# Chunked attention with a gated feed-forward: batch 0 in wide rows turned on the tensor engine, eight heads per step, shared PSUM banks and a hand-written order

## The chip, the cores and the metric

The kernel runs on one core of one Trainium2 chip. The metric is the device time in microseconds (us) of one execution. Each execution has a state: "fast" or "slow" (more than 1.5% above the fastest of the same kernel), and "unknown" for a kernel that ran only once. The profile is of one execution and has its own clock, and all moments below are us from the start of its span. The profile of the kernel before has a span 4 us below the median of the times in the table.

## The reference

There are two stages. The first is an attention in chunks of 32 tokens; each chunk sees 16 tokens to its left, itself, 8 tokens to its right, and 8 memory tokens. The second is a feed-forward layer (FFN below) with a ReLU gate.

```python
# q, k, v: [4 batches, 8 heads, 768 tokens, 64], float32; mem_k, mem_v: [4, 8, 8, 64]
for c in range(768 // 32):
    q_c    = q[:, :, 32*c : 32*c+32]
    k_full = concat(mem_k, k[:, :, max(0, 32*c-16) : min(768, 32*c+40)])
    v_full = concat(mem_v, v[:, :, same range])
    out[:, :, 32*c : 32*c+32] = softmax(q_c @ k_full.T / 8) @ v_full
x = out.transpose(0, 2, 1, 3).reshape(3072, 512)
y = (relu(x @ w_gate) * (x @ w_val)) @ w_out     # w_gate, w_val: [512, 1536]; w_out: [1536, 512]
```

## The kernel before

The 3072 tokens are cut into 8 blocks of 384; blocks 0 and 1 are batch 0. A block passes through these stations: q, k and v are loaded in float32; VectorE (DVE) casts them to 16 bits; one DMA transpose each makes kT and qT (head dimension on the partitions); the attention of four steps of 96 queries makes x; four DMA transposes make xT; then the FFN runs on TensorE (PE): twelve units of 4 gate and 4 value matmuls (384 columns each), then three output projections of 12 matmuls (512 columns).

```python
# PSUM: scores 2 banks, values 1, gate and value 4, output 1
sps = tile_pool(name="sps", bufs=2, PSUM); pps = tile_pool(name="pps", bufs=1, PSUM)
fps = tile_pool(name="fps", bufs=4, PSUM); ops = tile_pool(name="ops", bufs=1, PSUM)

def src(self, t, h0, nh, tok, parts):          # one token of one head: 64 floats = 256 bytes in a row
    return bass.AP(tensor=t.tensor, offset=t[self.b, h0, tok, 0].offset,
                   ap=[[D, parts], [S * D, nh], [1, D]])
def turn_k(self, h0, nh):                      # turn_q is alike
    nc.sync.dma_start_transpose(self.kT[...], self.kn[...])

# ... cut: start of the program ...
b0 = blocks[0]
for h0 in (0, 4):
    b0.load_k(h0, 4, sp); b0.load_q(h0, 4, nc.scalar.dma_start); b0.load_v(h0, 4, sp)
nc.gpsimd.tensor_copy(gate, b0.qf[:, 0, 4, 0:1])    # POOL waits for q, then issues all weights
for c in range(0, DFF, 512):
    pool(w_gate_sb[...]); pool(w_val_sb[...])
for c in range(0, NDC, 4):
    pool(w_out_sb[...])
# ... cut: casts, transposes and attention of block 0; load_all(blocks[1]) after its first four heads ...

# steady state: while the FFN of block n runs, block n+1 has its attention,
# block n+2 is loaded at the start, and cast and turned at units 8 to 13
for n in range(NBLK):
    ffn = ffn_units(blocks[n]); att = attention(blocks[n + 1], order)
    load_all(blocks[n + 2]); steps = prep_steps(blocks[n + 2])
    for u in range(len(ffn)):
        if 2 <= u < 2 + len(att): att[u - 2][1]()
        if u < len(att):          att[u][0]()
        ffn[u]()
        if u in steps:            steps[u]()
```

The raw tiles of q, k and v have two buffers each. The order on each engine is not simply that of the text: a scheduler sets it.

The softmax here doesn't subtract the row's maximum and nothing guards it: scores larger than these inputs give would overflow.

Of the kernel before, what the change touches and what calls it, by code (L numbers as in the profile page):

```python
# [7 lines left out]
F32 = mybir.dt.float32  # L8
F16 = mybir.dt.float16
BF16 = mybir.dt.bfloat16  # L10
# [6 lines left out]
def kernel(  # L17
# [18 lines left out]
    QB = 96  # L36
# [12 lines left out]
    MEMCOL = 400  # L49

    wpool = ctx.enter_context(tc.tile_pool(name="wpool", bufs=1))
    vpool = ctx.enter_context(tc.tile_pool(name="vpool", bufs=2))
    tpool = ctx.enter_context(tc.tile_pool(name="tpool", bufs=2))
    rpool = ctx.enter_context(tc.tile_pool(name="rpool", bufs=4))
    xpool = ctx.enter_context(tc.tile_pool(name="xpool", bufs=6))
# [3 lines left out]
    opool = ctx.enter_context(tc.tile_pool(name="opool", bufs=3))  # L59

    sps = ctx.enter_context(tc.tile_pool(name="sps", bufs=2, space=bass.MemoryType.PSUM))
    pps = ctx.enter_context(tc.tile_pool(name="pps", bufs=1, space=bass.MemoryType.PSUM))
    fps = ctx.enter_context(tc.tile_pool(name="fps", bufs=4, space=bass.MemoryType.PSUM))
    ops = ctx.enter_context(tc.tile_pool(name="ops", bufs=1, space=bass.MemoryType.PSUM))



    qn_t = [wpool.tile([128, HP, 2, NT, 2 * D], BF16, name=f"qn{i}") for i in range(2)]
    kf_t = [wpool.tile([128, 4, H, D], F32, name=f"kf{i}") for i in range(2)]
    vb_t = [wpool.tile([128, NJ, H, VW], F16, name=f"vb{i}") for i in range(3)]  # L70
    vf_t = [wpool.tile([128, NJ, H, D], F32, name=f"vf{i}") for i in range(2)]
    memv = wpool.tile([NMEM, B * H, D], F32, name="memv")
    ex_t = [wpool.tile([128, 4, 128], F16, name=f"ex{i}") for i in range(3)]
    for i in range(2):
        nc.vector.memset(kf_t[i][:, 3], 0.0)
    for i in range(2):
        nc.vector.memset(qn_t[i], 0.0)
    for t in vf_t:
        nc.gpsimd.memset(t[0:NMEM], 0.0)
    for t in ex_t:  # L80
        nc.gpsimd.memset(t[:, :, QB:128], 0.0)
    for t in vb_t:
        nc.gpsimd.memset(t[:, :, :, D:VW], 1.0)
# [3 lines left out]

    def build_mask(name, qb):

        m = wpool.tile([128, QB], F16, name=name)  # L90
        nc.gpsimd.memset(m, 1.0)
        bs = q_band_start(qb) - NMEM
        for g in range(QB // 32):
            c = 3 * qb + g
            lo = max(32 * c - 16, 0) - bs
            hi = min(32 * c + 40, S) - bs
            sl = m[:, 32 * g:32 * g + 32]
            if lo > NMEM:
                nc.gpsimd.affine_select(
                    out=sl, in_=sl, pattern=[[0, 32]], compare_op=ALU.is_ge,  # L100
                    fill=0.0, base=-lo, channel_multiplier=1,
                )
            if hi < 128:
                nc.gpsimd.affine_select(
                    out=sl, in_=sl, pattern=[[0, 32]], compare_op=ALU.is_ge,
                    fill=0.0, base=hi - 1, channel_multiplier=-1,
                )
        nc.gpsimd.memset(m[0:NMEM], 1.0)
        return m
# [6 lines left out]
    w_gate_sb = wpool.tile([128, NFC, DFF], F16, name="w_gate_sb")  # L116
    w_val_sb = wpool.tile([128, NFC, DFF], F16, name="w_val_sb")
    w_out_sb = wpool.tile([128, NDC, DM], F16, name="w_out_sb")

    class Block:  # L120


        def __init__(self, n):
            self.n, self.b, self.T = n, n // 2, n % 2
            self.kbase = 0 if self.T == 0 else MB - 16
            self.starts = [q_band_start(NJ * self.T + j) for j in range(NJ)]
            self.qn, self.kf = qn_t[n % 2], kf_t[n % 2]
            self.vb = vb_t[n % 3]
            self.qf = vpool.tile([128, NT, H, D], F32, name="qf")
            self.vf = vf_t[n % 2]  # L130
            self.kn = vpool.tile([128, HP, 4, 2 * D], BF16, name="kn")
            self.qT = tpool.tile([128, HP, 2, NT, 128], BF16, name="qT")
            self.kT = tpool.tile([128, HP, KCOLS], BF16, name="kT")
            self.kb = tpool.tile([128, HP, NJ, 128], BF16, name="kb")
            self.xT = None

        def src(self, t, h0, nh, tok, parts):
            return bass.AP(
                tensor=t.tensor, offset=t[self.b, h0, tok, 0].offset,
                ap=[[D, parts], [S * D, nh], [1, D]],  # L140
            )

        def load_k(self, h0, nh, dma):
            hs = slice(h0, h0 + nh)
            for t in range(3):
                dma(self.kf[:, t, hs, :], self.src(k, h0, nh, self.kbase + 128 * t, 128))  # L146
            dma(self.kf[0:16, 3, hs, :], self.src(k, h0, nh, self.kbase + 384, 16))
            dma(self.kf[16:24, 3, hs, :], bass.AP(
                tensor=mem_k.tensor, offset=mem_k[self.b, h0, 0, 0].offset,
                ap=[[D, NMEM], [NMEM * D, nh], [1, D]]))  # L150

        def load_q(self, h0, nh, dma):
            hs = slice(h0, h0 + nh)
            for t in range(NT):
                dma(self.qf[:, t, hs, :], self.src(q, h0, nh, MB * self.T + 128 * t, 128))

        def load_v(self, h0, nh, dma):
            hs = slice(h0, h0 + nh)
            for j in range(NJ):
                dma(self.vf[NMEM:128, j, hs, :], self.src(v, h0, nh, self.starts[j], BAND))  # L160

        def cast_k(self, h0, nh):
            p0, p1 = h0 // 2, (h0 + nh) // 2
            nc.vector.tensor_copy(
                self.kn[:, p0:p1], self.kf[:, :, h0:h0 + nh, :].rearrange("p t (a x) d -> p a t (x d)", x=2))

        def cast_q(self, h0, nh):
            p0, p1 = h0 // 2, (h0 + nh) // 2
            view = self.qf[:, :, h0:h0 + nh, :].rearrange("p t (a x) d -> p x a t d", x=2)
            for x in range(2):  # L170
                nc.vector.tensor_copy(self.qn[:, p0:p1, x, :, D * x:D * x + D], view[:, x])

        def cast_v(self, h0, nh):
            nc.vector.tensor_copy(self.vb[:, :, h0:h0 + nh, 0:D], self.vf[:, :, h0:h0 + nh, :])  # L174
            m = memv[:, H * self.b + h0:H * self.b + h0 + nh, :]
            m4 = bass.AP(tensor=m.tensor, offset=m.offset, ap=[m.ap[0], [0, NJ], [D, nh], [1, D]])
            nc.gpsimd.tensor_copy(self.vb[0:NMEM, :, h0:h0 + nh, 0:D], m4)  # L177

        def turn_k(self, h0, nh):
            p0, p1 = h0 // 2, (h0 + nh) // 2  # L180
            nc.sync.dma_start_transpose(  # L181
                self.kT[:, p0:p1].rearrange("p a (t c) -> p (a t) c", c=128),
                self.kn[:, p0:p1].rearrange("p a t c -> p (a t c)"))

        def turn_q(self, h0, nh):
# [20 lines left out]

    n_exp = [0]

    def quad_stages(blk, j, g, x_big):
        st = {}  # L210

        def scores():
# [179 lines left out]
```

## Time and profile before

| | before |
|---|---|
| time, median of 2 runs | 298.62 us (297.70 to 299.54) |
| span of the profile | 294.4 us |
| first gate matmul of block 0 | 72.2 us |
| first gate matmul of block 2 | 131.2 us |
| first gate matmul of block 4 | 184.4 us |
| a middle block | 26.2 to 26.9 us |

The page of the profile cuts the span into 40 equal slices (7.4 us each). A digit is the busy share of a slice in tenths; "DMA" is the mean over the 16 DMA engines; "GB/s" is what they moved. Three lines of it, and the line of the busiest group: line of the kernel, engine, operation, output and inputs, count, busy time in us, mean ns of one, and the idle time before them with what ended it.

```profile
PE   0000002147999799989999999999999499999983
...
DMA  9999999997929877899499989969896611111001
GB/s 166 217 197 187 195 145 207 233 181 168 218 51 171 207 163 157 135 243 239 92 205 246 217 121 237 225 136 193 223 245 119 139 71 28 29 51 59 0 36 71
...
L269 PE MATMUL g_ps<-xT,w_gate_sb 128*128 128x384 f16 x384 | 81.9, 328 | 0.4 <-DMA xT<-x_big 0.4
```

There are two regimes. For the first ten slices DMA is full and PE almost idle; then PE is full and DMA nearly so, until the loads end around slice 31. What PE waited for (total us, times, longest us) shows the same: the first scores waited until 44.8 us for the transposed q.

```profile
PE s_ps L215 <- DMA qT<-qn_94: 47.6, 3, 44.8
PE o_ps L231 <- DVE x_big L236: 10.7, 6, 7.4
```

Each line is a stretch of the span: its length, then for each engine the busy time and the number of instructions, the granted clock, the DMA share, and GB/s. The DMA share is worked out from the time that packets took. In a crowded stretch they took longer: the median of the 256-byte packets of SP's queue is 31 ns from 16 to 40 us, with the weights of POOL's queue beside them, and 18 ns from 52 to 76 us, without. There the share can come out above 1 (1.23 in the second line below).

```profile
core 0: us, PE busy (x) PEld busy (x) DVE busy (x) ACT busy (x) POOL busy (x), PEclk, DMA share, GB/s
0.00:184.40 184.40, 118.45 (x781) 66.80 (x782) 88.27 (x223) 51.50 (x103) 27.88 (x50) 0.99 0.97 184
22.00:38.00 16.00, 0.00 (x0) 0.10 (x1) 1.26 (x4) 0.00 (x0) 1.52 (x4) 1.00 1.23 191
131.20:158.10 26.90, 26.25 (x181) 15.00 (x180) 16.30 (x44) 11.48 (x24) 1.89 (x1) 1.00 0.91 199
```

From 22 to 38 us the share is 1.23, so a crowded stretch hides idle time elsewhere. A plainer count comes from the packet records of the kept trace (it is not a view of the page): up to 184.4 us at least one packet was under way for 165.9 us, and none for 18.5 us.

### The profile page before, as it was taken

To read this page: it belongs to the slowest core of one execution; us is meant where nothing else is said; L and a number is where in the kernel's file an instruction comes from. 1 tells how busy PE (TensorE), PEld (TensorE's weight loads), DVE (VectorE), ACT (ScalarE), POOL (GpSimd) and SP (SyncE) were. 2 spreads that over 40 slices of the span, in tenths; PEclk is the share of its full clock that TensorE was granted. 3 is DMA by queue.
4 is the path that set the end of the run, shared out by engine and by line. 5 is a ranking of instruction groups with operands and counts; after the bars stand their busy time and mean duration, and the time that the engine had idled before them with its cause. 6 is when DMAs were issued, how large, how long until landed. Compare 5 with 4: busy or idle time off the path is not lost.

```text
span 294.4 us, 4093 instructions
## 1 busy us (share of the span) xinstructions
PE 219.2 (74%) x1440; PEld 123.4 (42%) x1440; DVE 140.4 (48%) x355; ACT 92.9 (32%) x185; POOL 31.7 (11%) x52
## 2 busy tenths in 40 slices
PE   0000002147999799989999999999999499999983
PEld 0000001024554266546545654664565256545641
DVE  4400103675584079429924971884398127612310
ACT  1000002023342165236424622642453136423411
POOL 7950200020002000200020020002002000000000
PEclk9999999999999799999999999999999999999999
DMA  9999999997929877899499989969896611111001
GB/s 166 217 197 187 195 145 207 233 181 168 218 51 171 207 163 157 135 243 239 92 205 246 217 121 237 225 136 193 223 245 119 139 71 28 29 51 59 0 36 71
DMA packets 146152, 45.82 MB, mean 156 GB/s; under 512 B 138436, under 2 KB 143044, under 8 KB 146132
## 3 DMA queue, kind: packets, MB, share of 16 engines
q1 hardware_dynamic: 138164, 39.99, 67.1%
q0 software_dynamic: 4800, 4.79, 9.7%
q10 hardware_dynamic: 3168, 0.79, 1.5%
q8 instruction: 11, 0.18, 0.2%
q14 instruction: 9, 0.07, 0.1%
HBM read 30.34 MB, written 6.29 MB: 124 GB/s over the span
## 4 chain that ended last, share of the span: by engine, by line
PE 62%; DMA 21%; SPq 8%; DVE 5%; issue 1%; ACT 1%; ACTq 0%; DVEq 0%
PE vl_ps L273 20%; PE g_ps L269 19%; PE out_ps L284 16%; DMA vf_101<-in_v_dram 5%; DMA qT<-qn_94 5%; DMA qT<-qn_95 5%; PE o_ps L231 4%; PE s_ps L215 4%; DMA qf<-in_q_dram 3%; SPq L146 3%; DMA kf_96<-in_k_dram 2%; SPq L187 2%; SPq L181 1%; DVE gvT L277 1%; DMA xT<-x_big 1%
## 5 line engine op out<-in xcount | busy, mean ns | idle before, releaser
L269 PE MATMUL g_ps<-xT,w_gate_sb 128*128 128x384 f16 x384 | 81.9, 328 | 0.4 <-DMA xT<-x_big 0.4
L273 PE MATMUL vl_ps<-xT,w_val_sb 128*128 128x384 f16 x384 | 80.1, 329 | 0.0
L277 DVE TENSOR_TENSOR gvT<-vl_ps,g_relu 128x384 f16<-128x384 f32 x96 | 53.3, 555 | 54.3 <-PE vl_ps L273 53.0
L284 PE MATMUL out_ps<-w_out_sb,gvT 128*128 128x512 f16 x288 | 67.5, 385 | 1.6 <-ACT o_sb L287 1.3
L215 PE MATMUL s_ps<-qT,kb 128*128 128x192 bf16 x128 | 23.1, 272 | 58.4 <-DMA qT<-qn_94 47.6
L276 ACT ACTIVATE g_relu<-g_ps 128x384 f16<-128x384 f32 x96 | 47.2, 492 | 49.0 <-PE g_ps L269 31.9
L273 PEld LDWEIGHTS <-w_val_sb 128*128 128x128 f16 x384 | 37.6, 98 | 24.6 <-issue 0.7
L284 PEld LDWEIGHTS <-gvT 128*128 128x128 f16 x288 | 28.5, 99 | 36.4 <-issue 6.6
L269 PEld LDWEIGHTS <-w_gate_sb 128*128 128x128 f16 x384 | 35.7, 98 | 18.8 <-issue 1.6
L215 PEld LDWEIGHTS <-kb 128*128 128x128 bf16 x128 | 11.6, 105 | 64.4 <-DVE kb L204 40.8
L287 ACT COPY o_sb<-out_ps 128x512 f32<-128x512 f32 x24 | 14.1, 587 | 63.1 <-PE out_ps L284 63.1
L236 DVE TENSOR_TENSOR x_big<-o_ps,rinv 96x256 f16<-96x256 f32 x64 | 26.7, 418 | 1.2
L222 ACT ACTIVATE ex_104<-s_ps 128x384 f16<-128x384 f32 x22 | 10.8, 493 | 46.0 <-PE s_ps L215 44.6
L222 ACT ACTIVATE ex_105<-s_ps 128x384 f16<-128x384 f32 x21 | 10.3, 492 | 21.8 <-PE s_ps L215 20.9
L222 ACT ACTIVATE ex_106<-s_ps 128x384 f16<-128x384 f32 x21 | 10.3, 492 | 12.6 <-PE s_ps L215 11.9
L177 POOL CAST vb_99<-memv 8x2048 f16<-8x2048 f32 x3 | 5.7, 1903 | 75.9 <-DVE vb_99 L174 75.9
L177 POOL CAST vb_98<-memv 8x1024 f16<-8x1024 f32 (+1 forms) x4 | 5.8, 1458 | 64.0 <-DVE vb_98 L174 64.0
L234 DVE RECIPROCAL rinv<-o_ps 96x4 f32<-96x4 f32 x64 | 11.0, 171 | 3.2 <-PE o_ps L231 2.9
L201 DVE COPY kb<-kT 128x1440 bf16<-128x1440 bf16 (+1 forms) x9 | 4.8, 531 | 15.6 <-DMA kT<-kn 15.6
L174 DVE CAST vb_98<-vf_101 128x1024 f16<-128x1024 f32 (+1 forms) x3 | 2.6, 868 | 15.9 <-DMA vf_101<-in_v_dram 15.9
L231 PEld LDWEIGHTS <-ex_105 128*128 128x128 f16 x84 | 4.9, 103 | 11.9 <-DVE x_big L236 10.5
L177 POOL CAST vb_100<-memv 8x2048 f16<-8x2048 f32 x2 | 3.8, 1886 | 54.1 <-DVE vb_100 L174 54.1
(65 smaller groups left out, 107.6 us busy)
## 6 DMA issues: line engine op xcount, KB each, us to landing
out_dram<-o_sb SPq DMA_DIRECT2D x24, 256.0 KB
qf<-in_q_dram SPq DMA_DIRECT2D x21, 256.0 KB
vf_102<-in_v_dram SPq DMA_DIRECT2D x16, 240.0 KB
kf_97<-in_k_dram SPq DMA_DIRECT2D x12, 256.0 KB
vf_101<-in_v_dram SPq DMA_DIRECT2D x12, 240.0 KB
kf_96<-in_k_dram SPq DMA_DIRECT2D x9, 256.0 KB
w_gate_sb<-in_moe_w_gate_dram POOLq DMA_DIRECT2D x3, 512.0 KB, 10.3
w_val_sb<-in_moe_w_val_dram POOLq DMA_DIRECT2D x3, 512.0 KB, 12.7
```

The source lines that it names most:

```text
L177: nc.gpsimd.tensor_copy(self.vb[0:NMEM, :, h0:h0 + nh, 0:D], m4)
L215: nc.tensor.matmul(s_ps[:, i], lhsT=blk.kb[:, 2 * g + i, j, :], rhs=blk.qT[:, 2 * g + i].rearrange("p x t c -> p x (t c)")[:, :, QB * j:QB ...
L222: nc.scalar.activation(e, s_ps.rearrange("p a x c -> p (a x) c"), ACT.Exp, scale=SCALE)
L231: nc.tensor.matmul(o_ps[:, i, :], lhsT=st["ex"][:, i, :], rhs=blk.vb[:, j, 4 * g + i, :], start=True, stop=True)
L234: nc.vector.reciprocal(rinv, o_ps[0:QB, :, D:D + 1])
L236: nc.vector.tensor_tensor(out=x_big[:, 256 * g:256 * g + 256].rearrange("p (h d) -> p h d", h=4), in0=o_ps[0:QB, :, 0:D], in1=rinv_b, op=A ...
L269: nc.tensor.matmul(g_ps, lhsT=w_gate_sb[:, f, 128 * m:128 * m + 128], rhs=blk.xT[:, f, :], start=(f == 0), stop=(f == NFC - 1))
L273: nc.tensor.matmul(vl_ps, lhsT=w_val_sb[:, f, 128 * m:128 * m + 128], rhs=blk.xT[:, f, :], start=(f == 0), stop=(f == NFC - 1))
L276: nc.scalar.activation(g_relu, g_ps, ACT.Relu)
L277: nc.vector.tensor_tensor(out=state["gvT"][:, m, :], in0=vl_ps, in1=g_relu, op=ALU.mult)
L284: nc.tensor.matmul(out_ps, lhsT=state["gvT"][:, m, 128 * t:128 * t + 128], rhs=w_out_sb[:, m, :], start=(m == 0), stop=(m == NDC - 1))
L287: nc.scalar.copy(o_sb, out_ps)
```

## The change

The intent is to shorten the 72 us before the first FFN matmul, and to leave fewer packets for the DMA engines:

- Batch 0 (blocks 0 and 1 for q and k, block 0 for v) is loaded in rows of 1536 bytes, six tokens of one head. Block 0 takes the first 64 (q) or 80 (k, v) partitions, and block 1 the rest of q and k later.
- PE turns q and k of batch 0 (96 small turns), and gathers v into its bands with matmuls against a stepped identity; the FFN input xT of block 0 is turned by PE too.
- An attention step treats 8 heads instead of 4.
- Gate, value and output products share PSUM banks 4 to 7 in turn.
- The order on each engine is that of the text. Blocks 0 and 1 run all their gate and value units before the first output projection, so that w_out is needed later.
- The raw tiles have one buffer each instead of two.

```diff
-    sps, pps, fps, ops = four PSUM pools of 2, 1, 4 and 1 banks        # (shortened)
+    ctx.enter_context(tc.manual_schedule())
+    PS = pspool.tile([128, 8, 512], F32, name="PS")
+    def bank():                                     # gate, value and output take turns
+        n = 4 + rot[0] % 4
+        rot[0] += 1
+        return n
+    raw = {c: wpool.tile([128, H, R6, D], F32, name=f"{c}raw") for c in "kqv"}
+    def rows6(t, h0, nh, p0, np_):                  # six tokens of a head: 1536 bytes in a row
+        return bass.AP(tensor=t.tensor, offset=t[0, h0, R6 * p0, 0].offset,
+                       ap=[[R6 * D, np_], [S * D, nh], [1, R6 * D]])
# ... cut ...
+    load6(sp, "k", k, 0, 4, 0, PA)                  # PA = 80 partitions
+    load6(act, "q", q, 0, 4, 0, 64)
+    load6(sp, "k", k, 4, 4, 0, PA)
+    load6(act, "q", q, 4, 4, 0, 64)
+    load6(sp, "v", v, 0, 4, 0, PA)
+    load6(sp, "v", v, 4, 4, 0, PA)
# ... cut ...
+    pool.tensor_copy(gate[0:64], raw["q"][0:64, 4, 0, 0:1])
+    load_w(0)
+    load_w(1)                                       # a third of the gate and value weights
# ... cut: POOL and DVE cast, PE turns q and k, four attention steps with gather_v(j),
#          whose last instruction is a POOL copy of mem_v, and the first half-units of the FFN ...
+    pool.tensor_copy(raw["k"][96:97, 0, 0, 0:1], w_val_sb[96:97, 0, 0:1])
+    load6(sp, "k", k, 0, 8, PA, 128 - PA)           # block 1, held back by the copy above
+    load6(sp, "q", q, 0, 8, 64, 64)
+    b1.load_v()
+    for g in range(2, DFF // FG):
+        load_w(g)                                   # the other weights, then w_out
# ... cut: blocks 0 and 1; load(2) after unit 2 of block 1 ...
+    for t in range(NT):
+        outp(0, t)
+        if t == 1:
+            prep(2, 0); prep(2, 1); prep(2, 2)      # casts and DMA transposes of block 2
+        if t == 2:
+            prep(2, 3); prep(2, 5)
+    s[0].scores(); s[0].soft(); s[0].mask()         # block 2's attention among outp(1, t)
+    outp(1, 0)
+    load(3)                                         # block 3's loads ...
+    s[0].values(); s[0].norm(); s[0].turn_dma(xTs[2])   # ... ahead of block 2's xT transposes
# ... cut ...
```

## The prediction

> **What bounds the kernel now.** The page's slices and the timeline show two regimes. Until 72.2 us no FFN matmul runs. In that stretch the 16 DMA engines are 90% busy or more: q, k, v of blocks 0 and 1 in 256-byte rows (the page: 138,436 of 146,152 packets under 512 B), the weights, and DMA transposes. The first score matmul waited for qT until 44.8 us (the waits), the FFN for xT until 72.2. From 72 us on PE is the bound: four 384-column matmuls take 0.65 us, twelve of 512 columns 2.6 us, so a block's FFN needs 12x1.3 + 3x2.6 = 23.4 us, and a middle block takes 26.2 us (the chain of waits: 158.1 to 184.5), with DMA at 0.95 there.
>
> **What changes.** Block 0 and block 1's k and q come in 1536-byte rows. The hardware queue takes 23 ns of one engine per packet (67.1% of 16x294 us over 138,164); the weights' queue moves 2 KB in about 95 ns. Estimate from these: 75 ns per 1536 B, so block 0's loads fall from 14.6 to 8.4 us. [...] 11 against 22 GB/s per engine. About 17 us of transposes leave the DMA engines for PE: 96 small turns, 24 gather matmuls of 512 columns (0.216 us each, 5.2 us) and PSUM copies on ACT and DVE (0.5 to 0.9 us each). About 8 us of PE are added. Both FFN inner phases of blocks 0 and 1 run before the first output projection, so w_out is needed later.
>
> **On the critical path.** Estimated: loads in at about 8 us, four weight issues (0.75 us each) hold POOL, whose casts of q end near 14 us; scores at 15 to 17; four attention steps of 2.5 us; first half FFN matmuls near 25 us instead of 72. But the other weights are issued only after POOL's last copy of this attention (about 25 us), and compete with block 1's loads: 25 us of DMA, then w_out 9 us. So PE starves in block 0 until about 50 us; block 1's inner phase ends near 70 to 75. Block 2 loads only once w_out is in (about 59 us), and its xT transposes stand behind block 3's loads (14.6 us) in the same queue. I expect block 2's FFN to start near 95 us (before: 131.2), so about 36 of the 47 us gained at the first matmul survive. After that no gain in rate: 5x26.2 + 23.5 + 3.5 us of tail, with 0 to 6 us of stalls in blocks 2 and 3.
>
> 95 + 131 + 23.5 + 3.5 + 2 = 255 us span; the time before was 4 us above its span: about **259 us**, range **247 to 272**. Faster by over 2%: 0.95; within 2%: 0.04; slower: 0.01.
>
> **Checks in the profile.** First gate matmul at 23 to 28 us; idle PE at 30 to 50 us waiting for weights or block 1's v; DMA slices low near 17 to 25 us; first output projection near 70 to 75 us; block 2's first gate matmul at 90 to 103 us, waiting for xT; middle blocks still 26 to 27 us; no kT, qT transposes before about 75 us.
>
> **What would make it wrong.** Faster (240 to 246): weights land sooner than the shared queue estimate, so PE does not starve in block 0. Slower (over 272): transposes behind loads stall every block, or four shared PSUM banks stall PE because out copies and gate copies wait for one another, pushing the block above 27 us.

DMA terms are estimates from the profile before: the 75 ns lie between the 23 and 95 ns that a packet of each queue took, and the 9 us of w_out are about a third of the 28.6 us of the weights' queue (9.7% of the span). The 17 us of transposes agree with a count made afterwards: in the kernel after SP's queue has 11,904 packets of 256 bytes fewer beyond those that became wide rows, which is 17 us at 23 ns on 16 engines.

## The result, and the profile after

| | before | after | predicted |
|---|---|---|---|
| time, median of 2 runs | 298.62 us | 313.82 us (313.21 to 314.43) | 259 us |
| span | 294.4 | 311.5 | 255 |
| first gate matmul, block 0 | 72.2 | 38.0 | 25 |
| first output projection | 90.3 | 98.3 | 70 to 75 |
| first gate matmul, block 2 | 131.2 | 139.2 | 95 |
| first gate matmul, block 4 | 184.4 | 205.7 | 149 |
| a middle block | 26.2 to 26.9 | 26.3 | 26 to 27 |

The 149 of the last column is worked out from the prediction: block 2 at 95, two blocks of 26.2 us and 2 us of stalls. At its first output projection the kernel before has done the gate and value units of block 0 only, the kernel after those of blocks 0 and 1. The output is correct, and the time is 5% longer: the ratio is 1.0503, with a 95% interval of 1.0409 to 1.0597. Ratios here and below are the mean time of one kernel's fast runs over the mean of the kernel before's fast runs of the same rounds, so they are not quite the ratios of the medians quoted.

The change does win 34 us at the first gate matmul. By block 2 they are lost and 8 more, by block 4 it is 21 us behind, and the end gives back 4. The slices of the page after (7.8 us each):

```profile
PE   1049982587599658319599599999999999999995
...
DMA  7990099992692656982996999799799792202002
GB/s 170 194 135 2 0 172 198 186 190 45 126 209 42 148 121 136 194 156 43 218 207 126 232 220 158 136 231 214 155 199 210 173 177 105 40 14 103 0 0 101
```

DMA has a hole in slices 4 and 5, where it moves 2 and 0 GB/s, and more holes up to slice 20, where PE has holes too. The two first slices read 170 and 194 GB/s: the wide rows did not come faster than the 256-byte rows before (166 and 217). The stages, in the columns explained above:

```profile
22.00:38.00 16.00, 14.60 (x70) 7.67 (x71) 5.62 (x11) 7.34 (x12) 2.41 (x4) 1.00 0.02 3
98.20:139.10 40.90, 21.18 (x122) 10.24 (x119) 10.39 (x20) 6.75 (x11) 1.88 (x1) 0.83 0.76 144
0.00:205.60 205.60, 141.94 (x941) 82.06 (x942) 91.31 (x174) 57.88 (x101) 39.59 (x62) 0.89 0.84 146
```

The last of these lines stands against the first one from before. In the plainer count, up to block 4 packets were under way for 157.2 us (165.9 before) and none for 48.4 us (18.5 before). The change took about 9 us of DMA time away and left the engines without a packet for 30 us more. The difference is the 21 us by which block 4 starts late.

The pieces of the chain of work that ended last (start, length, what) say where:

```profile
2.20 11.72 DMA qraw<-in_q_dram
...
38.92 11.55 DMA w_val_sb<-in_moe_w_val_dram
50.47 18.67 DMA vraw<-in_v_dram
...
106.68 6.07 DMA qT<-q
...
136.69 2.34 DMA xT<-x_big
...
147.26 6.07 DMA qT<-q
```

The queue of SyncE (SP), which issues nearly all loads, transposes and stores, in order of time (start, length of the issues, kernel line, operation, tiles, count):

```profile
2.98 0.65 SPq L305 DMA_DIRECT2D memv<-in_mem_v_dram  x1
38.26 0.32 SPq L133 DMA_DIRECT2D kraw<-in_k_dram  x1
38.62 0.72 SPq L133 DMA_DIRECT2D qraw<-in_q_dram  x1
39.44 15.22 SPq L256 DMA_DIRECT2D vraw<-in_v_dram  x4
...
101.65 2.96 SPq L222 DMA_DIRECT2D out_dram<-o_sb  x2
104.70 1.87 SPq L276 DMA_TRANSPOSE kT<-k  x1
106.68 4.28 SPq L280 DMA_TRANSPOSE qT<-q  x1
```

SP issues nothing from 3.6 to 38.3 us. What holds it is POOL's one-element copy into the raw k tile (line 437), which stands in POOL's order behind the four copies of mem_v; each of those waits for ScalarE (ACT), which waits for PE's gather:

```profile
26.58 0.60 POOL L392 CAST vb<-memv 8x512 f16<-8x512 f32 x1 [5.09 <-ACT vb L391]
...
37.38 0.60 POOL L392 CAST vb<-memv 8x512 f16<-8x512 f32 x1 [3.36 <-ACT vb L391]
38.05 0.19 POOL L437 CAST kraw<-w_val_sb 1x1 f32<-1x1 f16 x1
38.17 0.76 POOL L332 DMA_DIRECT2D w_gate_sb<-in_moe_w_gate_dram  x1
```

What PE waited for shifted accordingly, from the first transposed q to the later transposes:

```profile
PE PS L199 <- DMA xT<-x_big: 15.0, 2, 11.7
PE PS L352 <- POOL q L345: 14.1, 2, 10.9
PE PS L147 <- DMA qT<-q: 13.8, 3, 6.6
```

Three readings need care. First, each of PE's gathers (six matmuls of 512 columns) took 2.56 us, 0.43 us a matmul, where an output projection has 0.22 us a matmul of the same width (twelve in 2.59 us). PE ran at half speed there, although the column of the granted clock reads 1.00 for that stretch (in e14 below it reads 0.50 for the same stretch, and a gather took 2.56 us too). Second, the shared PSUM banks, which the prediction feared, cost almost nothing: the longest wait of an FFN matmul for the engine that empties a bank is 1.9 us, once in the whole span, and from block 4 on a block takes 26.26 us. Third, a moment in one profile has a spread of several us. Two experiments below, e3 and e15, change nothing ahead of the first output projection, and it comes at 98.3 us here, at 102.3 in e3 and at 104.1 in e15. Part of this is PE's speed: after a wait of 3.4 to 3.9 us, block 1's first four gate matmuls show 0.81 us in the timeline here and 1.44 us in both others. Lengths of stretches from a common point are therefore safer than moments.

### The profile page after: what moved, and what is told of

Read it like the earlier page. It is cut to its first block, busy times and chain, and to the rows that moved or that the text cites. A ratio compares the mean times of both kernels' runs of the same rounds, so it can differ in the third digit from the quotient of the medians.

```text
span 311.5 us, 4333 instructions
## 1 busy us (share of the span) xinstructions
PE 244.2 (78%) x1612; PEld 139.8 (45%) x1612; DVE 144.1 (46%) x273; ACT 97.2 (31%) x174; POOL 43.7 (14%) x64
## 3 DMA queue, kind: packets, MB, share of 16 engines
q0 software_dynamic: 7920, 4.72, 10.9%
## 4 chain that ended last, share of the span: by engine, by line
PE 65%; DMA 21%; DVE 5%; SPq 4%; POOL 2%; issue 1%; ACT 1%; ACTq 0%; DVEq 0%
PE PS L211 19%; PE PS L199 18%; PE PS L204 17%; DMA vraw<-in_v_dram 6%; DMA qT<-q 6%; PE PS L147 4%; DMA qraw<-in_q_dram 4%; DMA w_val_sb<-in_moe_w_val_dram 4%; PE PS L389 3%; PE PS L166 3%; DMA xT<-x_big 1%; DVE ex L162 1%; SPq L179 1%; SPq L256 1%; DVE x_big L175 1%
## 5 line engine op out<-in xcount | busy, mean ns | idle before, releaser
L206 DVE TENSOR_TENSOR gvT<-PS,g_relu 128x384 f16<-128x384 f32 (+1 forms) x100 | 53.9, 540 | 102.4 <-PE PS L204 99.2
L199 PE MATMUL PS<-xT,w_gate_sb 128*128 128x384 f16 (+1 forms) x400 | 84.4, 337 | 16.6 <-DMA xT<-x_big 15.0
L204 PE MATMUL PS<-xT,w_val_sb 128*128 128x384 f16 (+1 forms) x400 | 83.9, 335 | 5.6 <-DMA w_val_sb<-in_moe_w_val_dram 3.7
L202 ACT ACTIVATE g_relu<-PS 128x384 f16<-128x384 f32 (+1 forms) x100 | 47.7, 477 | 75.2 <-PE PS L199 52.0
L211 PE MATMUL PS<-w_out_sb,gvT 128*128 128x512 f16 x288 | 66.3, 389 | 0.0
L199 PEld LDWEIGHTS <-w_gate_sb 128*128 128x128 f16 x400 | 39.5, 102 | 39.5 <-issue 20.0
L155 ACT ACTIVATE ex<-PS 128x768 f16<-128x768 f32 x32 | 25.9, 810 | 40.3 <-PE PS L147 38.5
L147 PE MATMUL PS<-qT,kb 128*128 128x192 f16 x128 | 18.6, 274 | 15.1 <-DMA qT<-q 13.8
L175 DVE TENSOR_TENSOR x_big<-PS,rinv 96x512 f16<-96x512 f32 x32 | 22.0, 686 | 1.1
L166 PE MATMUL PS<-vb,ex 128*128 128x66 f16 x256 | 14.0, 198 | 3.5 <-DVE ex L162 2.6
L162 DVE TENSOR_TENSOR ex<-ex,mask_int 128x768 f16<-128x768 f16 x24 | 14.2, 590 | 4.8 <-ACT ex L155 4.8
L172 DVE RECIPROCAL rinv<-PS 96x8 f32<-96x8 f32 x32 | 6.3, 197 | 12.1 <-PE PS L166 12.0
```

The costliest lines, as they stand in the source:

```text
L147: pe.matmul(PS[:, a // 2, 192 * (a % 2):192 * (a % 2) + 192].rearrange("p (x c) -> p x c", x=2), lhsT=self.kb[:, a, self.j, :], rhs=self.q ...
L155: act.activation(e.rearrange("p (b h) c -> p b h c", b=2), PS[:, 0:2, 0:384].rearrange("p b (h c) -> p b h c", h=4), ACT.Exp, scale=SCALE)
L162: dve.tensor_tensor(out=e, in0=e, in1=m8, op=ALU.mult)
L166: pe.matmul(PS[:, 2 + h // 4, VW * (h % 4):VW * (h % 4) + VW], lhsT=self.ex[:, h, :], rhs=self.vb[:, self.j, h, :], start=True, stop=True)
L175: dve.tensor_tensor(out=self.x.rearrange("p (b h d) -> p b h d", b=2, h=4), in0=o[:, :, :, 0:D], in1=rb, op=ALU.mult)
L199: pe.matmul(g_ps, lhsT=w_gate_sb[:, f, 128 * m:128 * m + 128], rhs=xTs[n][:, f, c0:c1], start=(f == 0), stop=(f == NFC - 1))
```

## The experiments

Theory 1, formed from this: the DMA engines decide the time until block 4, and the hand order starves them, because loads and weights are issued behind waits of POOL and transposes behind stores and loads. Rival: PE at half speed after its waits, or a late landing of q, sets the time. A third possibility came up later: that the wide rows did not shorten the DMA work at all. The experiments change the kernel after unless said otherwise; each ran beside the kernel before on the same chip (medians 298.46, 299.12, 298.42, 299.69 and 299.06 us).

### First call: single waits

**e1_weights_early.** Two more thirds of the first weights are issued before the attention.

```diff
     cast_v16(dve.tensor_copy, 4, 4, 0, PA)
+    load_w(2)
+    load_w(3)
...
-    for g in range(2, DFF // FG):
+    for g in range(4, DFF // FG):
```

> Edit: the third and fourth weight groups are issued on POOL right after its cast of v, before its four copies of memv, instead of after them. Theory 1 (the hand order issues DMA work behind waits, so the DMA engines idle from 22 to 38 us, and this lost DMA time is paid back until block 2): the DMA share of 22 to 38 us rises from 0.02 to about 0.4, block 1's v lands about 6 us earlier (69 to 63), block 2's first gate matmul moves from 139.2 to about 133 and the time falls by 4 to 7 us. Rival 2 (PE running at half speed after idle time is the loss): the time changes by less than 2 us, since the half-speed matmuls stay. Rival 3 (four shared PSUM banks): no change.

Measured: 314.66 us, ratio 1.0559 (1.0517 to 1.0601). The DMA share between 22 and 38 us rose from 0.02 to 0.58, but block 1's loads were still issued at 38 us, and block 2's first gate matmul came at 138.6 instead of 139.2. Up to block 4 no packet was under way for some 51 us, against 48 in the kernel after: the idle time only moved. No gain; the expectation failed. Filling half of the hole with something that was not waited for at the next step is worth nothing.

**e2_q_first.** The v loads move to ACT's queue behind q, so q has the engines to itself.

```diff
-    load6(sp, "v", v, 0, 4, 0, PA)      # both halves
+    load6(act, "v", v, 0, 4, 0, PA)
```

> Edit: block 0's v is loaded from the ACT queue behind q, not from the SP queue beside it. Theory 1: q lands near 9 us instead of 13.97, everything chained to it moves up by about 4 us (first gate matmul 38.0 to 34, block 2's first gate 139.2 to 135), and the time falls by 3 to 5 us. If v's later landing then delays the gather, the gain shrinks to 0 to 2 us. Rival 2: no more than the shift either; it cannot tell these apart.

Measured: 316.47 us, ratio 1.0642 (1.0587 to 1.0697). q landed at 12.4 instead of 14.0 us and the first gate matmul came at 35.2 instead of 38.0; block 2's came at 139.5. A gain of 3 us at the start does not show at block 2, nor in the time. This too was a miss for any theory in which the start alone counts.

**e3_xt_first.** Block 3's loads are issued after block 2's xT transposes instead of before.

```diff
     outp(1, 0)
-    load(3)
...
     s[3].values(); s[3].norm(); s[3].turn_dma(xTs[2])
+    load(3)
```

> Edit: block 3's loads are issued after block 2's four xT transposes instead of before three of them. If the transposes' place behind the loads in the one SP queue is a loss of its own: block 2's first gate matmul moves from 139.2 to about 131 and the time falls by about 7 us. Theory 1 (DMA work is what is late, its order inside the queue only moves the wait): block 2 starts at about 131, but block 3's q transpose lands about 8 us later (153 to 161), and the time stays within 3 us.

Measured: 312.51 us, ratio 1.0469 (1.0401 to 1.0536). Block 2's wait for xT fell from 11.7 to 3.3 us and its first gate matmul from 139.2 to 133.7, but block 3's wait for qT rose from 3.4 to 7.0 us, and block 4 began at 204.8 instead of 205.7. A wait in one queue was moved to another place. Not all of it: this profile had reached the first output projection, ahead of the edit, 4.0 us late, and needed 102.5 us from there to block 4, where the kernel after needed 107.4. The times, 312.51 and 313.82 us, are not told apart.

**e4_warm.** Fifty matmuls of 416 columns on 80 partitions in PE's first wait, to raise its speed before it is needed.

```diff
         b0.bands(a0, 2)
+        if a0 == 0:
+            for _ in range(50):
+                pe.matmul(PS[:, 7, 0:416], lhsT=step6[:, 0:128], rhs=step6[:, 0:416], start=True, stop=True)
```

> Edit: 50 matmuls of 416 columns that nothing reads fill PE's idle time between the turn of k and the turn of q (7.8 to 18.7 us). Rival 2: the matmuls that gather v then take 0.22 us instead of 0.43 per 512 columns, the first gate matmul moves from 38.0 to about 32.5, and the time falls by 5 us or more. Theory 1: the same shift of 5 us, because this stretch is a PE chain on the critical path, but all half-speed matmuls later (58 to 66, 139 to 143, 153 to 159 us) stay, and the time falls by at most 5.5 of the 15 us lost against before.

Measured: 324.76 us, ratio 1.0903 (1.0855 to 1.0951). They took 17.5 us, 0.35 us each, at half speed to the end, and delayed the first gate matmul by 5.6 us. Block 2 came 10.6 us and the end 10.9 us later, which is more than the delay put in; the rest is within the spread named above. The intended test failed. A delay put in at the start does not fade on the way.

### Second call: block 1's loads, and the rates

**e5_b1_early.** The small POOL copy and block 1's three loads move up, ahead of the gathers.

```diff
     cast_v16(dve.tensor_copy, 4, 4, 0, PA)
+    pool.tensor_copy(raw["k"][96:97, 0, 0, 0:1], w_val_sb[96:97, 0, 0:1])
+    load6(sp, "k", k, 0, 8, PA, 128 - PA)
+    load6(sp, "q", q, 0, 8, 64, 64)
+    b1.load_v()
...
-    (the same four lines, after the first half-units of the FFN)
```

> Edit: the loads of block 1 (k, q in wide rows, v in 256-byte rows) and the POOL copy that gates them come right after POOL's cast of v, before its memv copies; the weights stay late. Theory 1 (late DMA issue, with a chain block-1 loads, attention 1, block-2 loads, attention 2 behind it): block 1's v lands near 37 us instead of 69, the idle DMA stretch of 22 to 38 us is filled, weights land near 55, block 1's xT lands 10 us earlier than 82.6, block 2's first gate matmul moves from 139.2 to about 128, and the time falls by 7 to 12 us. If the start of block 2 is held by something else, as the first four runs leave possible: less than 3 us.

Measured: 302.89 us, ratio 1.0179 (1.0077 to 1.0281), 11 us below the kernel after, as theory 1 expected. The hole closed: the DMA share between 22 and 38 us is 0.94.

```profile
22.00:38.00 16.00, 14.60 (x70) 7.68 (x71) 5.62 (x12) 7.36 (x12) 2.30 (x4) 1.00 0.94 152
0.00:194.90 194.90, 139.49 (x940) 81.81 (x941) 89.81 (x174) 57.76 (x101) 39.08 (x62) 0.91 0.87 154
```

Block 0's first gate matmul did not move (38.15), block 2's moved from 139.2 to 126.2, and block 4's from 205.7 to 194.9. So the place of four lines cost 11 us by the medians (3.1% by the ratios to the kernel before), and not the speed of PE in that stretch, which is the same.

**e6_b1_and_weights_early.** e5 and e1 together.

```diff
     cast_v16(dve.tensor_copy, 4, 4, 0, PA)
+    load_w(2)
+    load_w(3)
+    (the four lines of e5)
```

> Edit: both the loads of block 1 and the third and fourth weight groups come before POOL's memv copies. Theory 1: the weights alone gave nothing because block 1's loads then held the chain; together they should give more than the sum: block 2's first gate matmul at 120 to 126, the time 10 to 16 us below the changed kernel. Rival (PE at half speed and in-order waits absorb what is won early): within 4 us of the changed kernel.

Measured: 302.10 us, ratio 1.0118 (1.0032 to 1.0203). This is not told apart from e5. The expectation of more than e5 was not met.

**e7_warm_dense.** As e4, but 36 matmuls of 512 columns of real k data (80 partitions); one run, state unknown.

```diff
+            for _ in range(36):
+                pe.matmul(PS[:, 7], lhsT=k16[0:PA, 0, 0, :], start=True, stop=True,
+                          rhs=k16[0:PA, 0].rearrange("p t c -> p (t c)")[:, 0:512])
```

> Edit: as in the run with 50 idle-time matmuls, but 36 of 512 columns that multiply the real k by itself (80 rows, no zeros) instead of the almost empty shift matrix. If busy time alone sets PE's speed: 0.43 us each all along, as the 50 were slow for 17 us. If the data or the share of active rows counts: after some 4 us they fall to 0.22 us each, while the gather's matmuls fall back to 0.43 within some microseconds. Time no better than the changed kernel by more than 3 us in either case.

Measured: 323.24 us. The 36 took 15.55 us, 0.43 us each, at half speed all along (see e13 for the line). The "some 4 us" of the expectation lies within what the kernel after shows, where the gate and value matmuls were slow for about 3 to 6 us from 139, 153 and 179 us on.

**e8_rates.** After the last output, k of batch 0 is loaded again in wide rows, twice each on 128, 80 and 64 partitions, and then twice in six loads of 256-byte rows. A one-element POOL copy marks each landing. One run, state unknown, lengthened on purpose by these loads.

```diff
+    for np_ in (128, 80, 64):
+        for _ in range(2):
+            load6(sp, "k", k, 0, 8, 0, np_)
+            pool.tensor_copy(gate[0:np_], kr[0:np_, 7, 5, 63:64])
+    for _ in range(2):
+        for t in range(R6):
+            sp.dma_start(kw[:, t], src(k, 0, 128 * t, 128))
+        pool.tensor_copy(gate, kw[:, 5, 7, 63:64])
```

> Edit: after the last output, when the DMA engines are idle, k of batch 0 is loaded again and again, each time with a POOL copy that waits for it: 1536-byte rows on 128, 80 and 64 partitions (1.57, 0.98, 0.79 MB), then the same 1.57 MB in six loads of 256-byte rows. My prediction's step (wide rows move 2 times the bytes per second): 1.57 MB in about 5 us after the 2 us of latency against 9 to 10 us in narrow rows. What the first 14 us of the changed kernel suggest (about 195 GB/s whatever the row): 8 us against 9 us. If the number of partitions limits: 80 and 64 partitions take as long as 128 or nearly.

Measured, the stretch in which each load's packets ran: the second load on 128 partitions, the first on 80, the second on 64, and both loads in 256-byte rows, which ran without a gap between them (the columns are those of the stages above; the last two are the DMA share and GB/s).

```profile
320.80:325.90 5.10, 0.00 (x0) 0.00 (x0) 0.00 (x0) 0.00 (x0) 0.00 (x0) 0.50 0.95 308
327.60:332.60 5.00, 0.00 (x0) 0.00 (x0) 0.00 (x0) 0.00 (x0) 0.00 (x0) 0.50 0.89 197
348.20:352.60 4.40, 0.00 (x0) 0.00 (x0) 0.00 (x0) 0.00 (x0) 0.00 (x0) 0.50 0.87 179
354.10:369.00 14.90, 0.00 (x0) 0.00 (x0) 0.00 (x0) 0.00 (x0) 0.18 (x1) 0.50 1.25 211
```

The packets took 5.1 us for 128 partitions (1.57 MB), 5.0 us for 80 (0.98 MB) and 4.4 us for 64 (0.79 MB). The time hardly depends on the number of partitions: 308 GB/s became 197 and 179. A packet of 1536 bytes took 65 ns on 128 partitions, 108 to 113 on 80 and 118 to 120 on 64 (medians of the packet records). POOL's marks lie further apart (6.9, 6.7 to 6.8, and 6.6 us), because each interval also holds the time from issue to the first packet and from the last packet to the mark, 1.7 to 2.2 us together. The short rows moved 211 GB/s. So in this run wide rows on 128 partitions were about 1.5 times as fast as short rows, and on 64 or 80 partitions no faster than short rows: block 0's share of k costs nearly as much as the k of both blocks. Why is not shown. My prediction had counted only the length of a row.

### Third call: the order further on

**e9_turn2_first.** e6, and block 2's casts and transposes are issued before block 0's output projections.

```diff
     for t in range(NT):
+        if t == 0:
+            prep(2, 0); prep(2, 1); prep(2, 2); prep(2, 3)
         outp(0, t)
-        if t == 1:
-            prep(2, 0); prep(2, 1); prep(2, 2)
```

> Edit, on top of the run with block 1's loads and two weight groups early (302 us): block 2's casts and its k and q transposes are issued before block 0's three output projections, not behind the stores of the first two. Theory 1: the q transpose lands before PE is done with block 0's projections, so PE's wait of 6.7 us for qT at about 95 to 102 us goes to 0 to 1 us, block 2's first gate matmul moves from 126 to about 119, and the time falls by 4 to 7 us. Rival (the wait only moves to xT behind block 3's loads): block 2's first gate moves by less than 3 us.

Measured: 294.10 us over all its runs; ratio of the fast ones 0.9778 (0.9683 to 0.9872), so better than the kernel before. Its profile fell in the slow state; block 2's wait for qT fell from 6.7 to 2.0 us.

**e10_split3.** e9, and block 3's k and q are loaded right behind qT of block 2, its v after xT of block 2; the stores of blocks 0 and 1 go to ACT's queue.

```diff
             prep(2, 0); prep(2, 1); prep(2, 2); prep(2, 3)
+            nats[3] = Nat(3); nats[3].load_k(); nats[3].load_q()
...
-    load(3)
...
     s[3].values(); s[3].norm(); s[3].turn_dma(xTs[2])
+    nats[3].load_v()
...
-            sp.dma_start(out[r0:r0 + 128, :], o_sb)
+            (act if n < 2 else sp).dma_start(out[r0:r0 + 128, :], o_sb)
```

> Edit, on top of e9_turn2_first: block 3's k and q loads are issued directly behind block 2's q transpose, its v behind block 2's xT transposes; stores of blocks 0 and 1 go to the ACT queue; one more output buffer. Theory 1 (DMA idle time before block 2 is what is lost, and loads in front of xT must have been started early enough): the idle DMA time between 82 and 113 us shrinks from about 13 to under 6 us, the wait for xT before block 2 from 11 to under 4 us, block 2 starts near 108 to 112, and the time falls by 6 to 10 us against e9_turn2_first, below the kernel before. If DMA work is the bound and idle time is not: less than 3 us.

Measured: 292.56 us over all its runs, ratio of the fast ones 0.9768 (0.9676 to 0.9861), no clear gain over e9. The profile is again of a slow run: the wait for xT of block 2 fell from 10.8 to 3.3 us, the wait for its qT rose from 2.0 to 6.4. The expectation failed in the way of e3.

**e11_pool_loads.** e9, with the loads of blocks 3 to 7 issued by POOL instead of SP.

```diff
     def load(n):
+        ld[0] = pool if n > 2 else sp
...
-                sp.dma_start(self.kf[:, t], src(k, self.b, self.kbase + 128 * t, 128))
+                ld[0].dma_start(self.kf[:, t], src(k, self.b, self.kbase + 128 * t, 128))   # q and v alike
```

> Edit, on top of e9_turn2_first: the loads of blocks 3 to 7 are issued from POOL, so the xT transposes no longer stand behind them in the SP queue. If the single queue's order is the loss: the wait for xT before block 2 falls from 11 to about 4 us and the time by 5 us or more. If the 16 engines' work is the bound: the loads and the transposes share them, the wait falls by half at most, and the time stays within 3 us; POOL's slower issue may even cost.

Measured: 298.77 us over all its runs; two of the four are slow, and the fast ones took 294.52 and 296.36. Ratio of the fast ones 0.9894 (0.9794 to 0.9994). Block 2 began 10 us earlier than in e9 (114.0), but block 4 only 3.5 us (187.9 against 191.4, which is of a slow run): the scores of block 4 waited 12.1 us for qT. In the kernel before, SP's packets took 31 ns beside POOL's weights and 18 ns without (given above); how much of e11's wait is due to such sharing is not shown. For POOL's slower issue there is one pair: the load of mem_v took POOL 0.85 us to issue in the kernel before, and SP 0.65 us in the kernel after.

**e12_wide_all.** e10, with batch 0's k and q loaded on all 128 partitions at once, so that block 1 needs no k and q loads of its own; v behind q on ACT's queue; DVE casts q; block 1's turns one unit earlier.

```diff
-    load6(sp, "k", k, 0, 4, 0, PA)
-    load6(act, "q", q, 0, 4, 0, 64)
+    load6(sp, "k", k, 0, 4, 0, 128)
+    load6(act, "q", q, 0, 4, 0, 128)
...
-    load6(sp, "k", k, 0, 8, PA, 128 - PA)
-    load6(sp, "q", q, 0, 8, 64, 64)
```

> Edit, on top of e10_split3: k and q of batch 0 are loaded on all 128 partitions at once (so block 1's k and q need no load of their own), v stands behind q, DVE casts q, and block 1's casts and turns come one step earlier. From the measured loads (6.6 to 6.9 us whether 64, 80 or 128 partitions are filled): q still lands at 12 to 14 us, block 1's wide loads (some 6 us of DMA) vanish, first gate matmul at about 33 instead of 38, block 2's first gate another 4 to 6 us earlier, time 3 to 6 us below e10_split3. If my reading is wrong and time goes with bytes: q lands at 17 us or later and nothing is won.

Measured: 287.08 us, ratio 0.9601 (0.9531 to 0.9671). In the first 14 us DMA moved 263 GB/s, where the kernel after moved 193, and the whole q of both blocks had landed at 14.0 us, just when block 0's share alone had landed before.

```profile
0.00:14.00 14.00, 1.78 (x28) 1.52 (x28) 6.93 (x16) 1.84 (x3) 3.48 (x21) 1.00 0.90 263
0.00:179.20 179.20, 138.06 (x940) 80.90 (x941) 90.34 (x176) 58.03 (x101) 38.91 (x59) 0.93 0.90 167
```

Up to block 4 packets were under way for 152.6 us, against 157.2 in the kernel after. This is a part of the saving that the wide rows had been meant to bring. The run makes several edits at once, so its gain in time is not that of the rows alone; their rate is shown by e8 and by the first line here.

### Fourth call: PE's speed

**e13_warm_ones.** The kernel after, with 36 matmuls of ones, 128 by 128 against 128 by 512, in the place of e7.

```diff
+    def spin(n, bk):
+        for _ in range(n):
+            pe.matmul(PS[:, bk], lhsT=ones[:, 0:128], rhs=ones, start=True, stop=True)
...
+        if a0 == 0:
+            spin(36, 7)
```

> Edit: the changed kernel with 36 matmuls of 512 columns in the same idle stretch of PE as in the two earlier runs of this kind, but of a 128x128 block of ones by a 128x512 tile of ones, so that all 128 rows work. If the share of active rows is what decides: after some 4 us they fall to 0.22 us each (the two earlier runs, on 80 rows, stayed at 0.35 and 0.43 per matmul to the end). Rival 2 then expects the gather's matmuls to run at 0.22 too, the first gate matmul at 33 and a time 5 us lower; theory 1 expects at most the same 5 us. If they too stay at half speed, something else than rows and data holds PE back in the first 20 us, and the time rises by 5 us or more.

Measured: 317.81 us, ratio 1.0618 (1.0567 to 1.0668). Here PE did reach full speed. The line of e7, then that of e13:

```profile
7.70 15.55 PE L380 MATMUL PS<-k 80*128 80x512 f16 x36
```

```profile
7.78 9.23 PE L368 MATMUL PS<-ones 128*128 128x512 f16 x36
```

If a matmul takes 0.43 us slow and 0.216 us fast, 9.23 us are about 7 slow and 29 fast ones, so full speed came after some 3 us, by this estimate. But three of the four gathers behind them took 2.77 us again in the timeline (2.76 in that of the kernel after) and only the last 1.81, and nothing was gained. The added matmuls of e7 and e4, on 80 rows, did not reach full speed: e7 stayed at half speed for 15.55 us, and e4 for 17.5 us of back-to-back matmuls.

**e14_fillers.** e12, with 12 to 38 such matmuls of ones in PE's waits: at the start, before the first gate matmul of blocks 1 and 2, and before the scores that wait for qT.

```diff
+    spin(38, 7)                                  # before block 0's turns
...
+        else:
+            spin(12, 0)                          # before block 1's first unit
...
+    spin(26, 0)                                  # before block 2's first scores
...
+            if (n, u) in ((2, 0), (2, 7), (3, 1)):
+                spin(14, 0)
```

> Edit, on top of e12_wide_all: such matmuls of ones (12 to 38) fill PE's waits at the start, before block 1's and block 2's first gate matmul, and before the score matmuls that wait for qT of blocks 2, 3 and 5. Rival 2 (half speed after each wait is a large part of the loss): the matmuls after these waits run at full speed at once, some 1.3 us saved at each and 5 us at the start, and the time falls 6 us or more below e12_wide_all (287 us). Theory 1: the next DMA landing sets the pace, so the time stays within 3 us of it.

Measured: 282.02 us, ratio 0.9434 (0.9355 to 0.9513), about 5 us below e12, between what the two theories expected. Up to block 4 PE has 119 more matmuls than in e12 and 18.1 us more busy time (156.15 against 138.06 us). At 0.216 us each the added ones alone would be 25.7 us, so the others took some 7 us less, by this estimate. The gathers did not get faster (2.56 us). So PE's half speed is a real cost, but a smaller one than the order.

### Fifth call: what holds blocks 2 and 3

In every version so far blocks 2 and 3 together took 64 to 74 us, where the kernel before took 53. In each, block 3's kT transpose was issued about 6 us after block 2's first gate matmul (145.3 after 139.2), where the kernel before had it 12 us ahead (119.1 before 131.2). So either this place in the order cost the 13 us, or DMA had no room.

**e15_turn3_after.** The kernel after, with block 3's casts and transposes right behind block 2's last xT transpose.

```diff
     s[3].values(); s[3].norm(); s[3].turn_dma(xTs[2])
+    prep(3, 0); prep(3, 1); prep(3, 2)
...
-                prep(3, u - 1)
+                prep(3, {2: 3, 4: 5}.get(u, -1))
```

> Edit of the changed kernel alone: the casts and the two transposes of block 3 (k and q) stand right behind block 2's last xT transpose instead of behind block 2's first FFN units. In every hand-ordered version so far block 3's kT transpose was issued about 6 us after block 2's first gate matmul (145.3 against 139.2), where the kernel before had it 12 us ahead (119.1 against 131.2). Theory 'order': the place in the order holds it; kT(3) issued at 138 to 140, the scores of block 3 wait 0 to 1 us for qT instead of 3.4, kT(4) at 164 to 168 instead of 170.0, time 3 to 6 us below the changed kernel. Rival 'DMA work': block 3's loads (issued until 130.7) and the xT transposes fill the DMA engines until 139 anyway; kT(3) moves by under 3 us, kT(4) by under 2, time within 2 us.

Measured: 311.57 us, ratio 1.0425 (1.0380 to 1.0470), not told apart from the kernel after (1.0409 to 1.0597). kT of block 3 came 1.2 us ahead of block 2's first gate matmul instead of 6.1 us behind, and blocks 2 and 3 together took 59.9 us instead of 66.5. But this profile had reached the first output projection, which lies ahead of the edit, 5.8 us late. From there to block 4 it took 99.1 us. The kernel after took 107.4, and e1, e2, e4, e5, e6, e7 and e13, which all have the old place, 105.9 to 108.7. So in this stretch the place was worth some 7 to 10 us, and the rival, DMA without room, does not hold for the kernel after: as block 2 began, its DMA engines were empty.

```profile
139.00:143.00 4.00, 3.84 (x15) 1.88 (x16) 0.56 (x1) 0.64 (x2) 0.00 (x0) 0.58 0.02 4
```

In blocks 2 and 3 no packet was under way for 9.0 us in the kernel after, and for 3.3 us in e15. The time itself fell by only 2 us, as the rival had expected. One run was profiled, and its first 104 us were slow ones; whether that is so in the other three is not known.

**e16_turn3_e12.** The same move on e12, where block 3's k and q are ready earlier.

```diff
     s[3].values(); s[3].norm(); s[3].turn_dma(xTs[2])
+    prep(3, 0)
     nats[3].load_v()
+    prep(3, 1); prep(3, 2)
...
-                prep(3, u - 1)
-                if u == 5: load(4)
+                prep(3, {3: 5, 6: 3}.get(u, -1))
+                if u == 6: load(4)
```

> The same move on the version with wide rows on 128 partitions, where block 3's k and q are loaded early (issued by 98.8): kT(3) right behind block 2's last xT transpose, v of block 3 next, then qT(3). Theory 'order': kT(3) at 112 to 114 instead of 118.8, scores(3) without the 6 us wait for qT, and block 4's first gate matmul 3 to 6 us earlier than 179.25; time 3 to 6 us below that version (287.1). Rival 'DMA work': kT(3) moves, but kT(4) stays within 2 us of 143.7 and the time within 2 us, because the DMA engines are full from there on.

Measured: 285.60 us, ratio 0.9534 (0.9489 to 0.9579). kT of block 3 came 8.9 us earlier (109.9 against 118.8), but kT of block 4 only 3.3 us (140.4), and block 4 began 2.3 us earlier (176.9). Blocks 2 and 3 took 65.8 us (66.3 in e12). In this stretch no packet was under way for 4.2 us in e12 and for 3.5 us here: unlike in the kernel after, the move found little room to fill, as the rival says.

**e17_steady4.** e16, with block 4's loads split and moved up as well, and its turns at units 10 to 14.

```diff
-                if u == 6: load(4)
-                prep(4, ...)                     # at units 12 to 14
+                if u == 3: nats[4] = Nat(4); nats[4].load_k(); nats[4].load_q()
+                if u == 6: nats[4].load_v()
+                prep(4, {10: 0, 11: 1, 12: 2, 13: 5, 14: 3}.get(u, -1))
```

> The run before, and block 4's loads split and moved up (k and q after block 2's unit 3, v after unit 6) with its casts and transposes at units 10 to 14. Theory 'order': kT(4) at 136 to 140 instead of 143.7, block 4's first gate at 171 to 175, blocks 2 and 3 together 60 to 63 us instead of 66.4 (before: 53.3), time 5 to 9 us below 287.1. Rival 'DMA work': no more than 2 us beyond the run before it.

Measured: 284.16 us, ratio 0.9511 (0.9453 to 0.9569), not told apart from e16. In its profile blocks 2 and 3 took 63.3 us.

**e18_steady4_fillers.** e17 with the fillers of e14 (the diff of e14 on e17).

> The run before plus the idle-filling matmuls of ones that took the wide version from 287.1 to 282.0. If the two gains are of different causes they add: 274 to 279. If fillers only hid the same waits, no better than 280 to 283.

Measured: 281.17 us, ratio 0.9415 (0.9350 to 0.9479), not told apart from e14, and so the gains of e17 and of the fillers do not add. Both versions beat both kernels.

### The ledger of DMA time

One account puts all this together: up to block 4's first gate matmul, for how long was at least one packet under way, and for how long none? The figures are counted from the packet records of the kept traces. By then every version after has moved 30.0 MB, and the kernel before 34.0 MB. A moment counts as busy even if one engine of 16 has a packet. The DMA share is given beside it; times the length it would make 161 us of work in e12, 168 in e14 and 174 in e18 for the same bytes, so that product is not a measure of the work. The lines for e14 and e18 read:

```profile
0.00:173.10 173.10, 156.15 (x1059) 88.87 (x1060) 90.67 (x177) 57.65 (x101) 38.48 (x59) 0.93 0.97 174
```

```profile
0.00:172.10 172.10, 152.10 (x1059) 86.00 (x1060) 91.41 (x177) 57.45 (x101) 37.40 (x59) 0.95 1.01 174
```

| kernel | block 4 begins | DMA share | packets under way | none under way | median time |
|---|---|---|---|---|---|
| before | 184.4 | 0.97 | 165.9 | 18.5 | 298.6 |
| after | 205.6 | 0.84 | 157.2 | 48.4 | 313.8 |
| e5: block 1's loads early | 194.9 | 0.87 | 155.4 | 39.5 | 302.9 |
| e12: order mended, rows on 128 partitions | 179.2 | 0.90 | 152.6 | 26.6 | 287.1 |
| e14: e12 with fillers | 173.1 | 0.97 | 152.1 | 21.0 | 282.0 |
| e18: e14 with blocks 3 and 4 turned earlier | 172.1 | 1.01 | 151.6 | 20.5 | 281.2 |

From block 4 to the end all versions after take 106 to 107 us. Of the 33 us by which e14 and e18 bring block 4 forward against the kernel after, 27 to 28 are time without a packet, and 5 to 6 are a shorter time with packets. In e14 and e18 little more idle time is left than in the kernel before. This agrees with the small gains of the moves on e12 in the last call.

## Why the prediction was right or wrong

What was right: a middle block stays at 26 to 27 us (26.26). No kT or qT transpose is issued before 75 us (104.7). There is a low stretch of DMA at the start, though at 22 to 38 us and not at 17 to 25. PE starves for block 1's v, block 2 waits for xT (11.7 us), and four shared banks do no harm beyond that.

What was wrong, in the prediction's own terms:

1. **"Block 0's loads fall from 14.6 to 8.4 us."** They took 14.0 (q landed at 13.97). The prediction priced a row by its length alone, at 75 ns. In the kernel after, the packets of 1536 bytes of k and v took 115 ns in this stretch and those of q 122 (medians); in e8 they took 65 ns on 128 partitions and about 120 on 64, and in e12 the same 14 us brought the q of both blocks. The "22 GB/s" behind the price did not show that long rows are faster: it counts the 2 KB of float32 that a weight packet reads. The page counts what lands, 4.79 MB in 4800 packets or 1.0 KB each, and that is 10.5 GB/s, no more than the 11 of the short rows. This put the start late, and block 1's k and q had to be paid again.
2. **"The other weights are issued only after POOL's last copy of this attention (about 25 us)."** The mechanism was right and the size was not: the copy ended at 38.0 us, since q came late, and since each gather took 2.56 us instead of the 1.3 us assumed. What stood behind it was sized wrongly too: not only weights, but also block 1's loads, and DMA idled 16 us. Moving block 1's loads alone (e5) gave back 11 us.
3. **"I expect block 2's FFN to start near 95 us."** It began at 139.2. This is the step that decided the direction. Of the 44 us, 13 come from the late first gate matmul, 13 more until the end of block 1's gate and value units (98.3 against 72.5, the middle of the predicted 70 to 75), and 18 between there and block 2, where transposes stood behind stores, and xT behind block 3's loads. e9's order alone took some 8 us or more off the time (302.1 to 294.1, medians of all runs; fast runs alone, ratio 1.0118 to 0.9778); from the first output projection to block 2 its profile, of a slow run, needs 34.4 us, where e6 needs 39.1.
4. **"0 to 6 us of stalls in blocks 2 and 3."** They were 13: 66.5 us against 53.2 before. With block 3's turns moved (e15) the two blocks took 59.9 us, so their place is about half of it. Most of the rest, some 6 us by an estimate, is PE at half speed after its waits at 139, 153 and 179 us, where four gate matmuls took up to 1.28 us instead of 0.65.

Behind these four lies one omission. The prediction followed the chain of waits and never added up the DMA work. The profile before shows packets under way for 166 us ahead of block 4. The prediction took away 6.2 us of block 0's loads and 17 us of transposes, which leaves 143 us, a few less if block 1's k and q are counted as well; its own times put block 4 at 149 us. That leaves the DMA engines some 6 us of idle time, where they had 18.5 before, and where the prediction itself expected a low stretch from 17 to 25 us. Measured, the change took away 9 us, no version fell below 151, and the kernel after had 48 us of idle.

What stays open: what decides PE's speed after a wait. The runs that stayed slow and those that did not differ in rows (80 and 128) and in data (e4 and e7 against the ones of e13), and no run varied one alone. Rows alone cannot be all of it: e13's last gather, on 80 rows, was partly fast (1.81 us), and the same 128-row matmuls of block 1 were fast in the kernel after and slow in e3 and e15. The single buffers of the raw tiles, which also tie loads to casts, were not tested by themselves.

## What to carry to other kernels

Before predicting an earlier start, add up the DMA work that must be done ahead of each milestone, and ask how much idle time the forecast leaves beside it. Count idle time in the packets and not from a share that can pass 1. When the order is written by hand, look for every DMA issue that stands in its queue behind an instruction that waits for something else; here the place of four lines cost about 11 us. In these runs a wide row paid only where the load also covered all partitions (e8: 308 GB/s on 128 partitions, 197 on 80 and 179 on 64, against 211 for short rows).
